# Attention and gated FFN on one core: the output tile moves into u's buffer, seven tiles for transposed scores, fetches asked for earlier, some squares on VectorE

## The chip, the cores and the metric

The kernel runs on one core of a Trainium2 chip. The metric is the device time of one execution in microseconds; smaller is better. The profile is of one execution, and its times are counted from the first instruction.

## The reference, cut to what matters

```python
# u, v: (4, 3136, 256)   z: (4, 3136, 64)   all float32
scores = (1 / S) * z @ z^T                  # per batch, S = 3136; symmetric
attn   = maximum(scores, 0) ** 2
x      = u * (attn @ v)                     # the input of the FFN
h      = maximum(x @ w_in, 0)               # 256 -> 1024
c      = conv over the sequence, 3 taps, per channel of h
out    = (h * sigmoid(c)) @ w_out           # 1024 -> 256
```

## The kernel before, in words

**Blocks and slots.** A batch of 3136 rows is cut into six query blocks of 512 (QB = 6, q = 0 to 5) and a rest of 64 rows. A block has 25 slots (NJ), one for each strip of 128 key rows. Four batches make 24 blocks and 600 slots; slot k lies in block k // 25. A slot makes a 128 x 512 tile of scores, squares its positive part, splits it into a rounded high part `ah` and a rest `al`, and TensorE multiplies both with v (`attend`, L431; six matmuls of 512 columns). The FFN of the block before runs in between (`ffn_*`, matmuls at L585 to L588 and L658 to L660).

**Three kinds of slot.** In a plain slot TensorE computes the scores (`scores`, L316 and L317, into the PSUM tile `s`), ScalarE takes the positive part into `t` (L391), VectorE multiplies the two (L402). A transposed slot uses that scores are symmetric: an earlier block has computed that tile, GpSimd has parted its words (`part`, L346), SP has written them to DRAM (`spill`, L359), and a transposing DMA brings them back into a tile `tp` (`fetch`, L367). There ScalarE squares `tp` twice: into the PSUM tile `s` (L388) and, rounded, into `ah` (L407); VectorE takes the difference (`al`, L155). The third kind are the four strips on a block's diagonal, at positions 1, 8, 15 and 22 of the block (2, 8, 15, 22 in the last block of a batch). The first of them is computed whole; the other three, called side pieces here, compute only the part right of the diagonal (384, 256 and 128 columns, L385) and get the part left of it by a transposing DMA from the DRAM tile `dd` of the same block (`fetch_side`, L375). The share of transposed slots grows with q: 16 of 25 in block 4 and 20 of 25 in block 5 of a batch.

**The order of the work** is written out by hand. In iteration k of the main loop the program issues, engine by engine and in this order: `split_hi` and `split_lo` of slot k+2, `relu` (with the squares above) of slot k+3, whatever the event table `ev` holds for k, `fetch` of slot k+LD, `fetch_side` of slot k+LE, `part` of slot k+2, `spill` of slot k+1, `attend` of slot k and `scores` of slot k+4. Each engine runs its own instructions in this order. All DMAs but two at the very end are issued by SP, one behind the other: one that must wait for a tile holds up all behind it.

**Rings of tiles.** The `tp` tiles form a ring of LB buffers, given out in the order of the program to `fetch` and `fetch_side` alike; a request gets the tile that was given out LB requests earlier and waits until that slot's last reader is done, which as a rule is `split_hi` of that slot, issued in iteration slot - 2. The PSUM tiles `s` are two: `scores` of slot k+4 must wait until `split_lo` (`al`, L155) has read the one given out two requests before. Of `ah` and `al` there are four each.

**u and the output.** `load_u` (L292) brings 512 KB of u for a block into the single tile `ut`; after the block's last slot `gate_x` multiplies the attention result into it (L553, L549) and `split_x` splits it for the FFN (`xh`, `xl`, L155 and L158). When the block's FFN is through, `evac` copies the output from PSUM into the single tile `ob` (ScalarE, L158), and `store` writes it out (L692). In the last blocks `tail` lists the work instead and orders it by its own costs; the rest of 64 rows of all batches (`r`) ends there with an `ob` of its own.

Of the kernel before, what the change touches and what calls it, by code (L numbers as in the profile page):

```python
# [8 lines left out]
F32 = mybir.dt.float32  # L9
# [5 lines left out]
AF = mybir.ActivationFunctionType  # L15
ALU = mybir.AluOpType
# [10 lines left out]


LA, LT, LS = 4, 3, 2
LD, LE, LP, LX, LB = 8, 5, 2, 1, 5  # L30
DG = [1, 8, 15, 22]


# [7 lines left out]
FS = [2, 5, 8, 11, 15, 18, 21, 24]  # L41
RELU, TAP, ST1, ST2, SIG, GATE, GHI, OUT0, OUT1 = 1, 2, 2, 3, 4, 4, 5, 10, 11
EVAC = 12
XS = 1

C_GATE, C_ST1, C_ST2, C_G, C_SIG, C_HI = 0, 2, 2, 2, 1, 3
# [22 lines left out]
def kernel(  # L69
# [10 lines left out]
    nc = tc.nc  # L80
# [4 lines left out]
    P = 128  # L85
    NB = 512
    QB = S // NB
# [3 lines left out]
    NJ = (S + P - 1) // P  # L91
    HALF = S - (NJ - 1) * P
    RW = B * (RQ + 3)
    NBLK = B * QB
    NS = NBLK * NJ
    DC = D // P
    FC = DFF // P
    SC1 = 2.0**-12
# [5 lines left out]
    wk = ctx.enter_context(tc.tile_pool(name="wk", bufs=1))  # L104
# [26 lines left out]
    def at_slot(k):  # L131
        blk, i = divmod(k, NJ)
        return blk, *ent[blk // QB][blk % QB][i]

    def side(k):
        blk, j, tr = at_slot(k)
        x = j - blk % QB * CB
        return x if blk and not tr and 0 <= x < CB else None
# [18 lines left out]
    def copy(eng, out, a):  # L157
        (eng.copy if eng is nc.scalar else eng.tensor_copy)(out, a)  # L158
# [128 lines left out]
    ut = {}  # L287
# [10 lines left out]
    sc, ah, al, pav = {}, {}, {}, {}  # L298

    def held(k):  # L300
        blk, j, _ = at_slot(k)
        return blk % QB == RB and j == NJ - 1
# [17 lines left out]
    rl, pl, dq, dd, tp = {}, {}, {}, {}, {}  # L320
# [57 lines left out]
    def relu(k):  # L378
        x = side(k)
        if at_slot(k)[2] or x or held(k):  # L380
            if held(k):
                tp[k] = rr.pop("s")
            if x:
                rl[k] = tp[k]
                nc.scalar.activation(tp[k][:, x * P :], sc[k][:, x * P : NB], AF.Relu, scale=SC1)  # L385
            else:
                sc[k] = ps.tile([P, 512], F32, tag="s", name="s", bufs=2)
            nc.scalar.activation(sc[k][:, :NB], tp[k], AF.Square, scale=SC1**-0.5)  # L388
            return
        rl[k] = wk.tile([P, NB], F32, tag="t", name="t", bufs=3)  # L390
        nc.scalar.activation(rl[k], sc[k][:, :NB], AF.Relu, scale=SC1)  # L391
        if act_squares(k):
            nc.scalar.activation(sc[k][:, :NB], rl[k], AF.Square, scale=SC1**-0.5)


    def act_squares(k):
        return SQ0 <= k < SQ1 and k % 2 == 1
# [174 lines left out]
    ph, hb, cc, gg, po = {}, {}, {}, {}, {}  # L572
# [4 lines left out]
    def width(blk):  # L577
        return RW - 2 if blk == "r" else NB
# [85 lines left out]
    ob = {}  # L664
# [7 lines left out]
    def evac(blk, dcs=range(DC), engs=(nc.scalar, nc.scalar)):  # L672
        e = width(blk)
        if blk not in ob:
            if blk == "r":
                ob[blk] = wk.tile([P, DC, RW], F32, tag="ut", name="ob", bufs=1)
            else:
                ob[blk] = wk.tile([P, DC, NB], F32, tag="ob", name="ob", bufs=1)
        for dc in dcs:
            copy(engs[dc], ob[blk][:, dc, :e], po[blk][dc][:, :e])  # L680

# [19 lines left out]
    PRE, MID, VEC, POST, PE0, PE1 = range(6)  # L701

    def at(slot, cls, fn, *args):
        ev[slot][cls].append((fn, args))
# [3 lines left out]
    for q in zs[2:]:  # L708
        s = min(C0.index(j) for j in range(q * CB, min(q * CB + CB, NJ))) - LA - 3
# [10 lines left out]
    for b in range(1, B):  # L720
        k0 = (b * QB - 1) * NJ
        for q in range(QB + 1):
            s = k0 - (QB - 2 - q) * NJ + (12 if q % 2 == 0 else 4)
            if q == QB - 2:
                s = k0 + 6
            elif q == QB - 1:
                s = k0 + NJ + 6
            elif q == QB:
                s = k0 + 9
            if b == 1 and q < 2:  # L730
                s = (Q0 - QB) * NJ + NJ + k0 + 4 + 8 * q
# [3 lines left out]
        for j in range(0, NJ, 2):  # L735
            s = k0 + max(last[j] + 2, last.get(j + 1, 0) + 2, V0 + V1 * j // NJ)
            if j == NJ - 1:
                s = k0 + V0 - 2
# [5 lines left out]
    n = len(RN) - 1  # L744
    for b in range(B):
# [9 lines left out]
        for i in range(n + 1):  # L755
            s = k5 + (R_J + 2 * i if i < n else R_D + 1) + 1
# [16 lines left out]
    for i, (_, what, f) in enumerate(sorted(need)):  # L773
        s = WS[i]
# [3 lines left out]
    for n in range(4):  # L778
        at(W_C + n, POST, prep_w, n, "conv", 0)
    for blk in range(NBLK):  # L780
        at(blk * NJ + 6, POST, load_u, blk)

    def before_end(slot, *args):
        if slot < NS:
            at(slot, *args)

    for blk in range(NBLK - 1):
        k0 = (blk + 1) * NJ
        at(k0, C_GATE, gate_x, blk, G)
        at(k0 + XS, C_XS, split_x, blk, (V, G))  # L790
        for f in range(FC):
            s = k0 + FS[f]
            if s == NS - 1:
                break
            at(s, POST, ffn_halo, blk, f)
            at(s, PE1, ffn_in, blk, f)
            at(s + RELU, C_RELU, ffn_relu, blk, f)
            at(s + RELU, C_RELU, ffn_keep, blk, f)
            at(s + TAP, C_TAP, ffn_tap, blk, f)
            at(s + ST1, C_ST1, ffn_conv, blk, f, 1)  # L800
            at(s + ST2, C_ST2, ffn_conv, blk, f, 2)
            before_end(s + SIG, C_SIG, ffn_sig, blk, f)
            before_end(s + GATE, C_G, ffn_gate, blk, f, G)
            before_end(s + GHI, C_HI, ffn_hi, blk, f, A)
            before_end(s + GHI, PE1, ffn_lo, blk, f, G)
            before_end(s + OUT0, PE0, ffn_out, blk, f, 0)
            before_end(s + OUT1, PE0, ffn_out, blk, f, 1)
        if blk < NBLK - 2:
            at(s + EVAC, C_EV, evac, blk)
            at(s + EVAC + 1, POST, store, blk)  # L810
    at(NS - 2, POST, rem_x)

    def tail():
# [43 lines left out]
        def end(w, d, engs, ds):  # L857
            n = width(w)
            out = []
            for dc in range(DC):  # L860
                c = op(engs[dc], 90 + n, d[dc::2], evac, w, [dc], [E[e] for e in engs])
                out.append(c)
                if ds:
                    op(ds[dc], 60, [c], store_half, w, dc, nc.sync if ds[dc] == "S" else nc.scalar)
            if not ds:
                op("S", 60, out, store, w)
            return out
# [44 lines left out]
    with tc.manual_schedule():  # L912
# [12 lines left out]
        for k in range(-LA, NS):  # L925
# [3 lines left out]
            if early and 0 <= k + LT:  # L929
                relu(k + LT)  # L930
                square(k + LT)
# [4 lines left out]
            if not early and k + LT < NS:  # L936
                relu(k + LT)
                square(k + LT)
# [67 lines left out]
```

## Time and profile before

| | |
|---|---|
| time, median of 3 runs | 1557.33 us (1556.37 to 1557.98) |
| time of the profiled execution | 1555.86 us |
| its span, first to last instruction | 1554.1 us |
| TensorE busy | 1531.0 us (99% of the span), 6796 matmuls |
| ScalarE busy | 1243.2 us (80%) |
| VectorE busy | 1055.6 us (68%) |
| GpSimd busy | 802.6 us (52%) |
| granted TensorE clock | 1.00 |

A line of the groups of instructions gives source line, engine, operation, tile written <- tiles read, shape, count, then the busy time in us and the mean of one in ns, and last the idle time of the engine just before them with what ended it. A matmul's own duration (some 390 ns for 512 columns) overlaps with the next, so the idle time of TensorE is the figure to read there. In a timeline the bracket at the end of a line is the idle time just before that instruction and what ended it.

### The profile page before, as it was taken

Reading aid. Unit: us, or ns where it says so; the run is one execution under the profiler, and the core shown is the slowest. Engines: PE = TensorE matmul, PEld = TensorE weight load, DVE = VectorE, ACT = ScalarE, POOL = GpSimd, SP = SyncE. Lnnn points to the kernel's source line nnn. Section 1 sums busy time; section 2 is a strip of 40 time slices with the busy share of each in tenths; the row PEclk is TensorE's granted clock in tenths of the full one; section 3 lists DMA queues with packets and bytes.
Section 4 is the critical chain, followed back from the end, with each engine's and each line's share of the span. In section 5 each row is a group of like instructions: output and inputs, shape, how many; then the busy total and the mean of one; then the engine's idle time right before and its main releaser. Section 6 shows DMA issues by size and latency. Waiting matters only on the chain.

```text
span 1554.1 us, 22492 instructions
## 1 busy us (share of the span) xinstructions
PE 1531.0 (99%) x6796; PEld 1259.6 (81%) x6796; DVE 1055.6 (68%) x1632; ACT 1243.2 (80%) x2365; POOL 802.6 (52%) x1121
## 2 busy tenths in 40 slices
PE   8999999999999999999999999999999999999998
PEld 6778888787888888887788888888788888888887
DVE  8997766556677766655767766665577776665557
ACT  8888788788777877878878777787787777878877
POOL 7765544346655543444765544444486553443333
PEclk9999999999999999999999999999999999999999
DMA  6543566675444556658344465574843445567431
GB/s 207 151 138 98 126 156 143 125 160 126 149 126 124 146 117 137 157 106 180 122 138 128 119 147 129 124 165 102 173 139 115 142 110 130 133 118 163 112 71 35
DMA packets 424650, 205.22 MB, mean 132 GB/s; under 512 B 317136, under 2 KB 404176, under 8 KB 424528
## 3 DMA queue, kind: packets, MB, share of 16 engines
q1 hardware_dynamic: 423856, 203.39, 53.3%
q8 instruction: 53, 0.87, 0.2%
q14 instruction: 69, 0.57, 0.1%
q10 hardware_dynamic: 672, 0.40, 0.1%
HBM read 36.59 MB, written 86.90 MB: 79 GB/s over the span
## 4 chain that ended last, share of the span: by engine, by line
PE 87%; ACT 6%; DMA 2%; POOL 2%; issue 1%; DVE 1%; SPq 0%; ACTq 0%; DVEq 0%; POOLq 0%
PE av L431 45%; PE ph L585 5%; PE ph L588 5%; PE ph L586 5%; PE o L660 5%; PE o L658 5%; PE o L659 5%; PE s L316 5%; PE s L317 4%; DMA tp<-dd 2%; PE av L498 2%; ACT s L388 1%; ACT ah L407 1%; ACT ph L622 1%; ACT hb L612 1%
## 5 line engine op out<-in xcount | busy, mean ns | idle before, releaser
L431 PE MATMUL av<-ah,vv 128*128 128x512 f32 x2400 | 736.7, 390 | 1.2 <-ACT ah L407 1.0
L155 DVE TENSOR_TENSOR al<-s,ah 128x512 fp32r<-128x512 f32 x576 | 397.0, 689 | 293.9 <-ACT ah L407 259.5
L431 PEld LDWEIGHTS av<-ah,vv 128*128 128x128 f32 x2400 | 449.7, 188 | 95.9 <-ACT re L509 1.7
L431 PE MATMUL av<-al,vv 128*128 128x512 f32 x1152 | 448.9, 390 | 0.5 <-DVE al L155 0.5
L155 POOL TENSOR_TENSOR gl<-hb,gh 128x512 fp32r<-128x512 f32 x192 | 248.2, 1293 | 166.0 <-ACT gh L158 165.8
L402 DVE TENSOR_TENSOR s<-s,t 128x512 f32<-128x512 f32 x295 | 205.5, 697 | 157.7 <-ACT t L391 156.7
L627 DVE SCALAR_TENSOR_TENSOR ph<-hb,cw,ph 128x512 f32<-128x512 f32 x384 | 286.6, 746 | 5.5 <-ACT ph L622 5.2
L346 POOL COPY pl<-t 128x1024 uint16<-128x1024 uint16 (+1 forms) x275 | 280.4, 1021 | 2.2 <-POOL hb L604 1.6
L431 PEld LDWEIGHTS av<-al,vv 128*128 128x128 f32 x1152 | 216.3, 188 | 47.2 <-DVE al L155 2.0
L391 ACT ACTIVATE t<-s 128x512 f32<-128x512 f32 x295 | 176.7, 599 | 93.6 <-PE s L317 84.6
L409 ACT CAST ah<-s 128x512 fp32r<-128x512 f32 x295 | 173.7, 589 | 72.9 <-DVE s L402 72.7
L388 ACT ACTIVATE s<-tp 128x512 f32<-128x512 f32 x301 | 179.3, 596 | 31.1 <-DMA tp<-dd 29.2
L617 POOL COPY halo<-hb 128x2 f32<-128x2 f32 x160 | 30.2, 189 | 318.9 <-ACT hb L612 318.9
L407 ACT ACTIVATE ah<-tp 128x512 fp32r<-128x512 f32 x301 | 188.7, 627 | 0.1
L316 PE MATMUL s<-zq,zh 128*128 128x512 f32 (+2 forms) x364 | 137.0, 376 | 16.1 <-DVE al L155 10.7
L585 PE MATMUL ph<-xh,wih 128*128 128x512 f32 x384 | 151.3, 394 | 0.6 <-DVE hb L641 0.6
L586 PE MATMUL ph<-xh,wil 128*128 128x512 f32 x384 | 150.0, 391 | 0.0
L658 PE MATMUL o<-gh,wol 128*128 128x512 f32 x384 | 149.5, 389 | 0.0
L659 PE MATMUL o<-gh,woh 128*128 128x512 f32 x384 | 149.5, 389 | 0.0
L660 PE MATMUL o<-gl,woh 128*128 128x512 f32 x384 | 149.4, 389 | 0.0
L634 ACT ACTIVATE ph<-ph 128x512 f32<-128x512 f32 (+1 forms) x200 | 115.4, 577 | 26.4 <-DVE ph L627 22.2
L641 DVE TENSOR_TENSOR hb<-ph,hb 128x512 f32<-128x512 f32 x192 | 131.8, 686 | 7.0 <-ACT ph L634 1.2
(117 smaller groups left out, 1871.5 us busy)
## 6 DMA issues: line engine op xcount, KB each, us to landing
dq<-pl SPq DMA_DIRECT2D x232, 256.0 KB, 2.8
vst<-in_v_dram SPq DMA_DIRECT2D x48, 256.0 KB, 3.3
ut<-in_u_dram SPq DMA_DIRECT2D x24, 512.0 KB, 4.2
out_dram<-ob SPq DMA_DIRECT2D x19, 512.0 KB, 3.3
st<-in_z_dram SPq DMA_DIRECT2D x24, 256.0 KB, 3.0
dd<-pl SPq DMA_DIRECT2D x23, 192.0 KB, 2.4
tp<-dq SPq DMA_TRANSPOSE x232, 3.7
dq<-pl SPq DMA_DIRECT2D x24, 128.0 KB, 2.4
```

The source lines that it names most:

```text
L155: eng.tensor_tensor(out=out, in0=a, in1=b.bitcast(F32), op=ALU.subtract)
L316: nc.tensor.matmul(s[:, c:], lhsT=zh[:, w], rhs=r, start=True, stop=False)
L346: nc.gpsimd.tensor_copy(pl[k], src.bitcast(U16).rearrange("p (n h) -> p h n", h=2))
L402: nc.vector.tensor_tensor(out=s, in0=s, in1=rl[k], op=ALU.mult)
L407: nc.scalar.activation(ah[k], tp.pop(k), AF.Square, scale=SC1**-0.5)
L431: nc.tensor.matmul(o, lhsT=w[:, j, d], rhs=r, start=first and i == 0, stop=last and i == len(ops) - 1)
L585: nc.tensor.matmul(o, lhsT=wih[:, dc, w], rhs=xh[blk][:, dc], start=(dc == 0), stop=False)
L586: nc.tensor.matmul(o, lhsT=wil[:, dc, w], rhs=xh[blk][:, dc], start=False, stop=False)
L627: nc.vector.scalar_tensor_tensor(out=c, in0=hb[blk, f][:, k : e + k], scalar=cw[:, f, k : k + 1], in1=c, op0=ALU.mult, op1=ALU.add,)
L658: nc.tensor.matmul(o, lhsT=wol[:, f, d], rhs=h, start=(f == 0), stop=False)
L659: nc.tensor.matmul(o, lhsT=woh[:, f, d], rhs=h, start=False, stop=False)
L660: nc.tensor.matmul(o, lhsT=woh[:, f, d], rhs=l, start=False, stop=(f == FC - 1))
```

## The change

The 4 KB per partition of `ob` are given up: `ob` becomes a tile of the ring `ut` (one buffer), and the two KB tiles of `tp` become seven instead of five. For that, `load_u` moves from slot 6 of its block to slot 18, and `store` from one slot behind `evac` to two. The output of the rest rows, which had used the ring `ut`, takes a tile of the ring `hb`. `fetch` is asked for ten slots ahead instead of eight, `fetch_side` six instead of five. In blocks 4 and 5 of each batch, for odd slots, VectorE computes the square of `tp` in place of ScalarE: `scalar_tensor_tensor` with both inputs `tp`; these are 80 instructions in all. TensorE and GpSimd keep their instructions in the same order.

```diff
-LD, LE, LP, LX, LB = 8, 5, 2, 1, 5
+LD, LE, LP, LX, LB = 10, 6, 2, 1, 7
 ...
+UL = 18
+DS = 4
 ...
-            nc.scalar.activation(sc[k][:, :NB], tp[k], AF.Square, scale=SC1**-0.5)
+            if by_vector(k):
+                nc.vector.scalar_tensor_tensor(
+                    out=sc[k][:, :NB], in0=tp[k], scalar=SC1**-1, in1=tp[k], op0=ALU.mult, op1=ALU.mult
+                )
+            else:
+                nc.scalar.activation(sc[k][:, :NB], tp[k], AF.Square, scale=SC1**-0.5)
 ...
+    def by_vector(k):
+        return k // NJ % QB >= DS and k % 2 == 1
 ...
             if blk == "r":
-                ob[blk] = wk.tile([P, DC, RW], F32, tag="ut", name="ob", bufs=1)
+                t = wk.tile([P, NB + 32], F32, tag="hb", name="or", bufs=3)
+                ob[blk] = t[:, : DC * RW].rearrange("p (a n) -> p a n", a=DC)
             else:
-                ob[blk] = wk.tile([P, DC, NB], F32, tag="ob", name="ob", bufs=1)
+                ob[blk] = wk.tile([P, DC, NB], F32, tag="ut", name="ob", bufs=1)
 ...
-        at(blk * NJ + 6, POST, load_u, blk)
+        at(blk * NJ + UL, POST, load_u, blk)
 ...
-            at(s + EVAC + 1, POST, store, blk)
+            at(s + EVAC + 2, POST, store, blk)
```

The first place is SP's queue in block 5 of the first batch, around the DMA of its second side piece, slot 140 (`tp<-dd` with 512 columns; the digits behind `dq` only tell DRAM tiles apart). Before:

```order
L359 DMA dd<-pl 256x1x256
L208 DMA vst<-in_v_dram 128x2x256
L521 DMA_TRANSPOSE rt<-do 128x4x256
L367 DMA_TRANSPOSE tp<-dq_386 128x1x1024 x2
L208 DMA vst<-in_v_dram 128x2x256
L367 DMA_TRANSPOSE tp<-dq_386 128x1x1024
L375 DMA_TRANSPOSE tp<-dd 128x1x512
L367 DMA_TRANSPOSE tp<-dq_386 128x1x1024
L692 DMA out_dram<-ob 128x2x512
```

And with the change:

```order
L361 DMA dd<-pl 256x1x256
L210 DMA vst<-in_v_dram 128x2x256
L531 DMA_TRANSPOSE rt<-do 128x4x256
L369 DMA_TRANSPOSE tp<-dq_384 128x1x1024 x2
L377 DMA_TRANSPOSE tp<-dd 128x1x512
L210 DMA vst<-in_v_dram 128x2x256
L369 DMA_TRANSPOSE tp<-dq_384 128x1x1024 x2
L210 DMA vst<-in_v_dram 128x2x256
L703 DMA out_dram<-ob 128x2x512
```

The side piece's DMA stands ahead of one more load of v and one more fetch, and the store of the output stands further behind it. The fetches ahead of it belong to slots two later than before.

The second place is VectorE at the start of that block 5. Before:

```order
L155 TENSOR_TENSOR al<-s,ah 128x512
L627 SCALAR_TENSOR_TENSOR ph<-hb,cw,ph 128x512
L155 TENSOR_TENSOR xl<-ut,xh 128x512
L155 TENSOR_TENSOR al<-s,ah 128x512
L627 SCALAR_TENSOR_TENSOR ph<-hb,cw,ph 128x512
L155 TENSOR_TENSOR al<-s,ah 128x512
L641 TENSOR_TENSOR hb<-ph,hb 128x512
```

And with the change:

```order
L157 TENSOR_TENSOR al<-s,ah 128x512
L391 SCALAR_TENSOR_TENSOR s<-tp 128x512
L637 SCALAR_TENSOR_TENSOR ph<-hb,cw,ph 128x512
L157 TENSOR_TENSOR xl<-ut,xh 128x512
L157 TENSOR_TENSOR al<-s,ah 128x512
L637 SCALAR_TENSOR_TENSOR ph<-hb,cw,ph 128x512
L157 TENSOR_TENSOR al<-s,ah 128x512
L391 SCALAR_TENSOR_TENSOR s<-tp 128x512
L651 TENSOR_TENSOR hb<-ph,hb 128x512
```

In every second slot the square `s<-tp` stands right behind a slot's `al` and ahead of the FFN's steps; ScalarE's queue loses the same squares (L388) at the same places.

## Rows read from the trace of the kernel before

**Rows 1.** The page, part 1: busy us (share of the span) and instructions.
```profile
PE 1531.0 (99%) x6796; PEld 1259.6 (81%) x6796; DVE 1055.6 (68%) x1632; ACT 1243.2 (80%) x2365; POOL 802.6 (52%) x1121
```
**Rows 2.** Waits of PE, whole span: us in total, times, longest us.
```profile
PE s L316 <- DVE al L155: 10.7, 9, 1.8
PE av L431 <- ACT ah L407: 1.0, 1, 1.0
```
**Rows 3.** The same view, stretch 65 to 130 us alone.
```profile
PE s L316 <- DVE al L155: 1.1, 2, 0.7
```
**Rows 4.** Timeline of PE, end of the first three batches: start, us, instruction, idle before.
```profile
354.99 0.33 PE L316 MATMUL s<-zq,zh 128*128 128x128 f32 x1 [1.52 <-DVE al L155]
364.06 0.50 PE L316 MATMUL s<-zq,zh 128*128 128x512 f32 x1 [1.76 <-DVE al L155]
...
735.38 0.33 PE L316 MATMUL s<-zq,zh 128*128 128x128 f32 x1 [1.70 <-DVE al L155]
743.77 0.50 PE L316 MATMUL s<-zq,zh 128*128 128x512 f32 x1 [1.07 <-DVE al L155]
...
1116.57 0.33 PE L316 MATMUL s<-zq,zh 128*128 128x128 f32 x1 [1.73 <-DVE al L155]
1124.60 0.50 PE L316 MATMUL s<-zq,zh 128*128 128x512 f32 x1 [0.72 <-DVE al L155]
```
**Rows 5.** Timeline of ACT in the same three places.
```profile
342.35 0.60 ACT L388 ACTIVATE s<-tp 128x512 f32<-128x512 f32 x1 [3.77 <-DMA tp<-dd]
358.95 0.60 ACT L388 ACTIVATE s<-tp 128x512 f32<-128x512 f32 x1 [2.55 <-DMA tp<-dd]
...
722.73 0.60 ACT L388 ACTIVATE s<-tp 128x512 f32<-128x512 f32 x1 [4.05 <-DMA tp<-dd]
738.66 0.60 ACT L388 ACTIVATE s<-tp 128x512 f32<-128x512 f32 x1 [1.87 <-DMA tp<-dd]
...
1103.90 0.60 ACT L388 ACTIVATE s<-tp 128x512 f32<-128x512 f32 x1 [5.55 <-DMA tp<-dd]
1119.49 0.60 ACT L388 ACTIVATE s<-tp 128x512 f32<-128x512 f32 x1 [1.51 <-DMA tp<-dd]
```
**Rows 6.** The page, part 5: groups of instructions.
```profile
L388 ACT ACTIVATE s<-tp 128x512 f32<-128x512 f32 x301 | 179.3, 596 | 31.1 <-DMA tp<-dd 29.2
L627 DVE SCALAR_TENSOR_TENSOR ph<-hb,cw,ph 128x512 f32<-128x512 f32 x384 | 286.6, 746 | 5.5 <-ACT ph L622 5.2
```
**Rows 7.** Timeline of SP, block 5 of the first batch.
```profile
338.60 1.20 SPq L375 DMA_TRANSPOSE tp<-dd  x1
```
**Rows 8.** DMA issues: count, KB each where known, median us to landing.
```profile
out_dram<-ob SPq DMA_DIRECT2D x19, 512.0 KB, 3.3
...
tp<-dd SPq DMA_TRANSPOSE x69, 3.0
```
**Rows 9.** Stretches: us, then busy us (x) of PE, PEld, DVE, ACT, POOL; clock, DMA share, GB/s.
```profile
312.00:375.00 63.00, 59.72 (x263) 48.56 (x262) 36.39 (x56) 52.20 (x101) 29.28 (x44) 1.00 0.65 142
```
**Rows 10.** Instructions on tile ut: duration ns min/median/max, first and last start.
```profile
L155 DVE TENSOR_TENSOR xl<-ut,xh x25: 676/691/694, 61.1 to 1509.9; 128x512 fp32r<-128x512 f32 x25
...
L549 POOL TENSOR_TENSOR ut<-x,ut x23: 1289/1296/1306, 57.7 to 1445.9; 128x512 f32<-128x512 f32 x23
L155 POOL TENSOR_TENSOR xl<-ut,xh x23: 1302/1467/1877, 61.1 to 1457.1; 128x512 fp32r<-128x512 f32 x23
...
DMA to landing us min/median/max: 3.7/4.2/6.1
```
**Rows 11.** Line 531, all of it: duration ns min/median/max.
```profile
L531 DVE SCALAR_TENSOR_TENSOR xr<-rt,ur x4: 343/348/363, 347.3 to 1486.6; 128x128 f32<-128x128 f32 x4
```
**Rows 12.** Timeline, block 4 of the second batch: PE at slot 265, VectorE before it.
```profile
654.18 0.28 PE L316 MATMUL s<-zq,zh 128*128 128x256 f32 x1
```
**Rows 13.** Timeline of DVE, the same place.
```profile
652.97 0.69 DVE L155 TENSOR_TENSOR al<-s,ah 128x512 fp32r<-128x512 f32 x1
...
655.00 0.69 DVE L155 TENSOR_TENSOR al<-s,ah 128x512 fp32r<-128x512 f32 x1 [0.68 <-ACT ah L407]
```

## The prediction
> **What bounds the kernel now.** I read the page first, then TensorE's waits, then the timelines of the places where it waits. TensorE is busy for 1531.0 of 1554.1 us [rows 1], and the change leaves its instructions as they are, so the only time to be had is TensorE's idle time. Most of what is recorded as a wait behind the program's start has one name: `scores` (L316) waits for `al` (L155), nine times, 10.7 us, and once `attend` waits for `ah`, 1.0 us [rows 2]. Two of the nine, 1.1 us, lie in the stretch from 65 to 130 us where the weights are prepared [rows 3]; the change hardly touches that. That leaves 10.7 - 1.1 + 1.0 = 10.6 us. Six of these waits come in pairs at the ends of the first three batches: 1.52 and 1.76, 1.70 and 1.07, 1.73 and 0.72 us, together 8.50 [rows 4].
>
> VectorE is late with `al` there because ScalarE was late with `ah`, and ScalarE was late because it stood still for a side piece: each pair on TensorE has a pair on ScalarE ahead of it, in which L388 waits for `tp<-dd` [rows 5]. The first of a pair is slot 15 of block 5 (3.77, 4.05, 5.55 us), the second slot 22 (2.55, 1.87, 1.51). The second ones fit to the hundredth: 2.55 - 1.76 = 0.79, 1.87 - 1.07 = 0.80, 1.51 - 0.72 = 0.79. So the engines are 0.8 us ahead there, and what a side piece is later than that TensorE loses. For the first ones it is 2.25 and 2.35; in the third batch, with the `ah` wait of 1.0 us counted in, about 2.8. All waits of L388 for side pieces make 29.2 us in the span [rows 6]; the 9.9 us not shown lie where TensorE was far enough behind, but for one in block 4 of the first batch that makes the seventh `al` wait, 9.6 - 8.50 = 1.1 us.
>
> **Why the side pieces are late.** One slot takes (743.77 - 364.06) / 150 = 2.53 us (those two are the scores of slots 150 and 300) [rows 4]. Take slot 140, the first pair's piece. SP asks for it in iteration 135. Five requests back in the ring is slot 138, and that tile comes free with `split_hi` in iteration 136; the piece is wanted by `relu` in iteration 137. So one slot, 2.53 us, is left for a DMA that ScalarE sees 342.35 - 338.60 = 3.75 us after its issue [rows 5, 7], and whose median landing is 3.0 us [rows 8]. Counting all 69 side pieces in this way, with SP's order, 12 have one slot and 57 have two; slot 22 of block 5 has two and is still late when SP lags.
>
> **The change, part by part.** *Ring of seven, fetches 10 and 6 ahead.* Slot 140 is asked for in iteration 134, gets the tile of slot 133 (free since iteration 131), and stands in SP's queue behind the fetch of slot 144, which needs the tile of slot 137, free in iteration 135. So it starts two slots ahead of its use instead of one. The same count for all 69 gives one slot more for 65 and two more for 4 (slot 22 of each block 4, where the seventh wait comes from). A slot is 2.53 us, so the first waits become 3.77 - 2.53 = 1.24, 1.52 and 3.02 us, the second ones 0.02, 0 and 0. Against the margins 2.25, 2.35 and 2.8 only the third batch could still lose, 0.2 us; against 0.8 none. Earlier fetches of `dq` tiles only lengthen a lead that shows no wait.
>
> *Squares on VectorE.* 80 x 0.596 = 47.7 us leave ScalarE [rows 6], about 10 squares or 6 us in each of eight blocks, three of them between slots 15 and 22, so the margin of the first waits grows by up to 1.8 us. VectorE's price shows nowhere in the trace: no such instruction has both inputs 512 columns wide in SBUF. From below it is the 0.69 us of `xl<-ut,xh`, two SBUF inputs of that size in a plain `tensor_tensor` [rows 10]; from above 4 x 0.348 = 1.39 us, since the one form that does match (L531) takes 348 ns for 128 columns [rows 11] and that includes a fixed part. I take 0.75, the same operation on 512 columns with PSUM operands [rows 6]. 80 x 0.75 = 60 us, 7.5 in a block in which VectorE is busy for 36.39 of 63 us [rows 9]; it lies beside TensorE's work and I cost it at nothing. If that cover were gone, the tightest place says what it costs: `al` ends at 652.97 + 0.69 = 653.66 and the scores that need it start at 654.18, 0.52 us later [rows 12, 13].
>
> *Output in u's ring, load_u at slot 18, store one later.* The new order is `gate_x` and `split_x` of one block (slots 0 and 1 of the next), `evac` at slot 11, `store` at 13, `load_u` at 18, use at 25. `evac` has ten slots of room. `load_u` waits for a store that lands in 3.3 us [rows 8] and was issued 5 slots, 12.7 us, before; its own landing takes 6.1 us at most [rows 10] of the 7 slots, 17.7 us, to its use. Nothing. The store one slot later keeps SP from standing at an `evac` that has not run yet; a small gain, already contained in the leads. In the tail, the last outputs wait for tiles that were free long before; nothing. Taking 512 KB out of the first 20 us may gain or lose some tenths; I put it at zero with 0.5 us on each side.
>
> **The sum.** 10.6 us of waits, less 0.2 that may stay in the third batch and 0.4 for new small waits, is 10.0 us. The profiled execution took 1555.86 us, so 1545.9 us; the median of the runs shown is 1.47 us above that execution, so I predict **1547.3 us**. About 0.2%, 3.1 us, is what a measurement of this kernel can tell from no change.
>
> **The rivals.** *Half of it stays.* The count above follows the tiles; SP must also keep up. Its transposing DMAs take 1.2 us of issue each [rows 7], and a fetch that stands ahead of a side piece now needs its own tile first. If the pieces gain half a slot only, the waits fall by 1.27 us: 2.50, 2.78 and 4.28 against margins of 2.25 to 2.8 plus what ScalarE is spared. Then the second waits, 1.28, 0.60 and 0.24, lose 0.5 once, and the first at most 0.25, 0.43 and 1.5. With some new waits of the squares this is 3 to 5 us left, 1550 to 1552 us. Chance 0.13.
>
> *ScalarE itself is short.* If it is not the DMA but ScalarE's load, 52.20 of 63 us in block 5 [rows 9], that makes TensorE wait, the pieces come earlier and the waits only change their name; with 6 us less to do it would still keep perhaps 2 us. 1555.5 us, within 0.2%. Against it stands the fit to 0.01 us with the DMA waits. That VectorE's added squares give back what the pieces gain comes out at the same time. Chance 0.08.
>
> *The squares collide with GpSimd: slower.* In the trace GpSimd's `xl<-ut,xh`, which runs beside VectorE's instruction on the same tiles, takes 1302 to 1877 ns, its `ut<-x,ut`, of the same kind and size, 1289 to 1306 [rows 10]; so an instruction with two SBUF inputs on VectorE can cost GpSimd up to 0.58 us. In the other direction, a square that starts behind a GpSimd instruction could stand for up to 1.3 us. The mechanism: square and wait, 0.75 + 1.3, push the next `al` back by 2.05 us; of that 0.52 us of margin and some 0.68 us in which VectorE waits for `ah` anyway [rows 12, 13] take up 1.2, and TensorE loses 0.85 at a slot that computes scores. From a delay of 1.2 us on it decides. At two such slots in each of 8 blocks that is 13.6 us, and 1547.3 + 13.6 = 1560.9 us. The Trainium skill ("SBUF — State Buffer", section "Who interferes with whom") states the rule: a VectorE instruction with two SBUF inputs contends with a GpSimd instruction that reads SBUF, and whichever comes second is blocked until the first is done. By that rule, the trace agrees for GpSimd as the second; no row here shows VectorE blocked for that long. Against it: GpSimd is busy for 29.28 of 63 us [rows 9], so most squares meet nothing or the end of something, and VectorE idles for over 26 us of those 63. Chance 0.04.
>
> **How the numbers follow.** The forecast has 0.75; the three rivals 0.13, 0.08 and 0.04. Around the forecast lie the half microsecond of the start on each side, the 0.6 taken off the waits, and 1 us by which the runs shown differ: 1544.5 to 1549.5 (below, if the 0.6 and the waits of the weight stage go too). To hold 8 in 10 the range takes in the half case: 1544.5 to 1553.0. Faster by over 0.2% is below 1554.2: the forecast and the half case, less a little, 0.86. Within 0.2%: 0.10. Slower: 0.04.
>
> **What would show it.** Right: `scores` waiting for `al` falls from 10.7 us to below 2, with nothing but the two waits in the weight stage and some tenths left; ScalarE's waits for `tp<-dd` fall from 29.2 us to below 8 (a part may turn up as waits of VectorE, which now squares slot 22's piece); a new group of 80 squares `s<-tp` on VectorE of 0.69 to 0.80 us; ScalarE's busy time is 48 us lower. Wrong: squares of over 1 us, or idle time ahead of them that ends with GpSimd; TensorE waiting for `al` at new places in blocks 4 and 5; `gate_x` waiting for the DMA of u; or the pairs of waits at the ends of the batches still there.

## The result and the profile after

The changed kernel takes 1541.16 us (median of 4 runs, 1540.89 to 1541.77) against 1556.85 us before: a ratio of 0.990, 95% interval 0.9883 to 0.9917, 15.7 us faster. The forecast was 1547.3 us with a range of 1544.5 to 1553.0: the direction was right, the gain 10.0 us instead of 15.7, and the time lies 3.3 us below the range. The profiled executions, 1555.86 and 1540.89 us, differ by 15.0 us, and that is the difference that can be taken apart.

TensorE's waits of the changed kernel, in the view of [rows 2] (us in total, times, longest):

```profile
PE s L318 <- DVE zq L157: 5.2, 1, 5.2
PE s L318 <- DVE al L157: 1.2, 2, 0.7
PE ph L595 <- DVE hb L651: 0.9, 1, 0.9
PE av L441 <- DVE al L157: 0.5, 1, 0.5
PE av L441 <- ACT x L558: 0.5, 1, 0.5
PE s L318 <- DVE wr L277: 0.2, 1, 0.2
```

Of the nine waits for `al` two are left, 1.2 us; they are the two of the weight stage [rows 3]. The first line is the start of the program. Neither ScalarE nor VectorE has a wait for `tp<-dd` left, where ScalarE had 29.2 us [rows 6]; ScalarE's squares, and the new ones of VectorE, as groups of instructions:

```profile
L395 ACT ACTIVATE s<-tp 128x512 f32<-128x512 f32 x221 | 132.2, 598 | 1.8
```

```profile
L391 DVE SCALAR_TENSOR_TENSOR s<-tp 128x512 f32<-128x512 f32 x80 | 65.6, 820 | 6.9 <-ACT tp L387 6.6
```

The first is the line of [rows 6] with 80 instructions and 47.1 us fewer, and no DMA ends its idle time any more. ScalarE's busy time as a whole fell by 38.8 us only, where 48 was foreseen, since the drawn bars of neighbours overlap. The second group took 820 ns on average, where 750 was assumed. The same six matmuls as in [rows 4], in the timeline of the changed kernel:

```profile
351.00 0.22 PE L318 MATMUL s<-zq,zh 128*128 128x128 f32 x1
358.04 0.39 PE L318 MATMUL s<-zq,zh 128*128 128x512 f32 x1
...
727.10 0.22 PE L318 MATMUL s<-zq,zh 128*128 128x128 f32 x1
734.13 0.39 PE L318 MATMUL s<-zq,zh 128*128 128x512 f32 x1
...
1103.15 0.22 PE L318 MATMUL s<-zq,zh 128*128 128x128 f32 x1
1110.19 0.39 PE L318 MATMUL s<-zq,zh 128*128 128x512 f32 x1
```

None has idle time in brackets. The distances to [rows 4] are 3.99, 6.02, 8.28, 9.64, 13.42 and 14.41 us: the gain comes mostly in steps at the ends of the batches, where the waits were. The stretch with the same 263 matmuls as in [rows 9], block 5 of the first batch, which now takes 3.8 us less:

```profile
309.69:368.85 59.16, 59.16 (x263) 48.73 (x262) 44.04 (x67) 47.03 (x90) 32.05 (x44) 1.00 0.64 142
```

TensorE is busy for all of it. VectorE went from 36.39 to 44.04 us, ScalarE from 52.20 to 47.03, and GpSimd from 29.28 to 32.05, though GpSimd has the same 44 instructions.

### The profile page after: what moved, and what is told of

Same layout as the page of the kernel before. It is cut to its first block, busy times and chain, and to the rows that moved or that the text cites. A ratio compares the mean times of both kernels' runs of the same rounds, so it can differ in the third digit from the quotient of the medians.

```text
span 1539.1 us, 22577 instructions
## 1 busy us (share of the span) xinstructions
PE 1526.2 (99%) x6796; PEld 1260.3 (82%) x6796; DVE 1110.6 (72%) x1712; ACT 1204.4 (78%) x2285; POOL 822.5 (53%) x1121
## 4 chain that ended last, share of the span: by engine, by line
PE 95%; DVE 2%; ACT 1%; issue 1%; DMA 0%; POOL 0%; DVEq 0%; ACTq 0%; POOLq 0%
PE av L441 50%; PE ph L595 6%; PE o L670 6%; PE o L668 6%; PE o L669 6%; PE ph L596 6%; PE ph L598 6%; PE s L318 5%; PE s L319 5%; PE av L508 1%; DVE s L412 0%; DVE al L157 0%; DVE ph L637 0%; ACT t L398 0%; DMA st<-in_z_dram 0%
## 5 line engine op out<-in xcount | busy, mean ns | idle before, releaser
L157 POOL TENSOR_TENSOR gl<-hb,gh 128x512 fp32r<-128x512 f32 x192 | 252.0, 1313 | 157.5 <-ACT gh L160 157.1
L622 ACT ACTIVATE hb<-ph 128x512 f32<-128x512 f32 x192 | 114.7, 597 | 40.3 <-PE ph L598 39.0
```

Of the source, the lines that this page charges most:

```text
L157: eng.tensor_tensor(out=out, in0=a, in1=b.bitcast(F32), op=ALU.subtract)
```

## The experiments

Theory A says that the gain comes from side pieces that are ready earlier; B, that it comes from ScalarE's squares; C, from the moved u, output and store; D, from fetches ten ahead. Each kernel was timed in three rounds beside the kernel before.

**Without the squares on VectorE.** `DS = 4` becomes `DS = 6`.

> The changed kernel with all squares of transposed tiles back on ScalarE. Theory A (the gain comes from the side pieces, which start one slot earlier): within 2 us of the changed kernel, 1541 to 1543 us, and ScalarE's waits for tp<-dd stay below 8 us. Theory B (ScalarE's load made TensorE wait, and the squares on VectorE are the gain): the pairs of waits at the ends of the first three batches come back, 1551 to 1556 us. Theory C (the freed order: output in u's ring, u loaded later, store later): 1541 us, as A.

1541.78 us (1541.08 to 1542.02), ratio 0.9905 [0.989, 0.992], and no wait for `tp<-dd`. B falls as the main cause: the squares are worth 0.6 us here by the medians, and the runs of the two kernels overlap.

**Side pieces five ahead.** `LE` from 6 back to 5.

> The changed kernel with the side pieces asked for five slots ahead as before; ring of seven, fetches ten ahead, squares on VectorE as changed. By the count of tiles 8 pieces have one slot again and 61 have two. Theory A: ScalarE or VectorE waits for tp<-dd again at slot 15 of block 5 (2 to 4 us each), and part of the gain goes: 1545 to 1553 us. Theory B: 1541 us. Theory C: 1541 us.

1541.18 us (1540.79 to 1542.96). A's number was wrong. The waits at slot 15 are back, but shorter than before, and TensorE feels little of them. ScalarE's waits in this run:

```profile
ACT s L395 <- DMA tp<-dd: 8.1, 4, 2.3
```

Four waits of some 2 us, all at slot 15 of block 5; at slot 22 none. In the ring of seven that piece takes the tile of slot 143, not 144, so the ring alone gives it a slot more. The count was right for slot 15 and had missed that for slot 22. TensorE in the first and the third batch, where ScalarE's waits are 2.08 and 2.32 us:

```profile
351.91 0.33 PE L318 MATMUL s<-zq,zh 128*128 128x128 f32 x1 [0.26 <-DVE al L157]
1104.96 0.33 PE L318 MATMUL s<-zq,zh 128*128 128x128 f32 x1 [0.52 <-DVE al L157]
```

Ahead of these two late `al` VectorE ran a square of 0.95 and 0.96 us, so the squares may have a part in them; how large a part was not tried.

**The old ring.** `LD, LE, LB` back to 8, 5, 5.

> The changed kernel with LD, LE and LB as before (8, 5, 5): what is left of the change are the squares on VectorE and the moves of u, output and store. Theory A: the waits for tp<-dd are back and most of the gain is gone, 1549 to 1556 us, better than before only by what ScalarE is spared. Theory B: 1541 us. Theory C: 1541 us.

1556.47 us (1553.07 to 1559.44, ten runs), ratio 0.9999 [0.9986, 1.0012]: nothing of the gain is left, though squares and moves are in, and A's range ends 0.5 us lower. Squares and moves together give nothing with the old ring; that could still be two effects of opposite sign, which the next two runs separate.

**The squares alone.**

```diff
-            nc.scalar.activation(sc[k][:, :NB], tp[k], AF.Square, scale=SC1**-0.5)
+            if k // NJ % QB >= 4 and k % 2 == 1:
+                nc.vector.scalar_tensor_tensor(
+                    out=sc[k][:, :NB], in0=tp[k], scalar=SC1**-1, in1=tp[k], op0=ALU.mult, op1=ALU.mult
+                )
+            else:
+                nc.scalar.activation(sc[k][:, :NB], tp[k], AF.Square, scale=SC1**-0.5)
```

> The kernel before with the 80 squares on VectorE and nothing else. Theory A: as the run with the old ring, 1549 to 1556 us. Theory B: 1541 us. Theory C: no gain, 1556 us; the distance to the run with the old ring is what the moves are worth.

1552.82 us (1550.6 to 1553.89), 0.9972 [0.9962, 0.9983]: 3.9 us of gain, while ScalarE and VectorE still wait for `tp<-dd`. So the squares make up for late pieces in part. That this is better than the run before, which has the moves as well, suggests that the moves cost some 3.7 us with the old ring.

**The moves alone.** The changed kernel with 8, 5, 5 and `DS = 6`.

> The changed kernel with the old ring and leads (8, 5, 5) and the squares back on ScalarE: only u's and the output's tile, u's load at slot 18 and the store one slot later are left. Theory A, as it stands after the first runs (the moves put u's load beside the side pieces and cost some 3 us as long as those have no room; ring and leads give the room): 1557 to 1561 us. Theory C (the moves are a gain of their own): 1541 to 1550 us.

1561.03 us (1560.19 to 1564.5), 1.003 [1.0018, 1.0041]: slower by 4.0 us. C is not only without gain, its sign is the other one.

**Fetches eight ahead.** `LD` from 10 back to 8.

> The changed kernel with fetches of transposed tiles eight slots ahead as before, ring of seven, side pieces six ahead: every side piece has at least four slots between its tile and its use. Theory A: 1540 to 1542 us, no wait for tp<-dd at all. A rival, D (it is the fetches ten ahead, tp<-dq, that gain): 1550 to 1556 us.

1540.55 us (1540.22 to 1541.03), one wait for `tp<-dd` of 0.3 us. D falls: the fetches ten ahead gain nothing.

**The kernel before with side pieces six ahead.** One number: `LE` from 5 to 6.

> The kernel before with one number changed: side pieces asked for six slots ahead instead of five; ring of five, fetches eight ahead. By the count of tiles slots 8 and 15 of block 5 get two slots instead of one, slot 22 of block 4 three, slot 22 of block 5 stays at two. Theory A (each piece late for itself): the first wait of each pair goes, the second stays, 1548 to 1551 us. Theory A2 (the second wait of a pair is the echo of the first, since SP and the ring stand still with ScalarE): both go, 1541 to 1546 us. Theory D: no gain, 1556 us.

1542.65 us (1542.2 to 1543.09), 0.9909 [0.9892, 0.9925]. One number in the old kernel gives 14.4 of the 15.7 us. The time lies in A2's range, not in A's. Its timeline of ScalarE at the places of [rows 5]:

```profile
338.34 0.60 ACT L388 ACTIVATE s<-tp 128x512 f32<-128x512 f32 x1 [1.25 <-DMA tp<-dd]
353.85 0.60 ACT L388 ACTIVATE s<-tp 128x512 f32<-128x512 f32 x1 [1.32 <-DMA tp<-dd]
...
715.59 0.60 ACT L388 ACTIVATE s<-tp 128x512 f32<-128x512 f32 x1 [2.03 <-DMA tp<-dd]
730.27 0.60 ACT L388 ACTIVATE s<-tp 128x512 f32<-128x512 f32 x1 [0.62 <-DMA tp<-dd]
...
1091.77 0.60 ACT L388 ACTIVATE s<-tp 128x512 f32<-128x512 f32 x1 [1.81 <-DMA tp<-dd]
1106.22 0.60 ACT L388 ACTIVATE s<-tp 128x512 f32<-128x512 f32 x1 [0.40 <-DMA tp<-dd]
```

At slot 15 the prediction had 1.24, 1.52 and 3.02 us for one slot more; measured are 1.25, 2.03 and 1.81. TensorE's waits for `al` are the two of the weight stage, 1.2 us. The 1.32 us at slot 22 cost TensorE nothing that the profile records, so the margin of 0.8 us is no constant; that it holds only behind a longer wait at slot 15, which has used up the lead, fits the rows but was not tried. The count of tiles gave slot 22 no slot more, and its wait fell all the same: asked for one iteration earlier, its DMA goes out ahead of the two stores `zq<-zh` and `zq<-zl` (at 349.88, they at 351.21 and 351.81), which before went ahead of it (353.73 and 354.31, it at 355.01).

**One side piece of each batch earlier.** The kernel before, with slot 15 of block 5 alone asked for six ahead.

```diff
-            if 0 <= k + LE < NS:
-                fetch_side(k + LE)
+            for d in (LE + 1, LE):
+                if 0 <= k + d < NS and (late_one(k + d) == (d > LE)):
+                    fetch_side(k + d)
...
+    def late_one(k):
+        return k // NJ % QB == RB and k % NJ == 15
```

> The kernel before, in which only the side piece at slot 15 of block 5 of each batch is asked for one slot earlier; four DMAs move in the whole program. Theory A: three waits of TensorE go (1.52, 1.70, and 1.01 + 1.73 us with what they cost beyond), 1549 to 1551 us. Theory A2: the second waits go as well, 1545 to 1547 us. Theory D: no gain, 1556 us.

1548.11 us (1546.66 to 1548.44), 0.9942 [0.9927, 0.9957], between the two expectations and nearer to A's. The first and the second wait of the first batch, on ScalarE:

```profile
340.82 0.60 ACT L391 ACTIVATE s<-tp 128x512 f32<-128x512 f32 x1 [2.07 <-DMA tp<-dd]
357.95 0.60 ACT L391 ACTIVATE s<-tp 128x512 f32<-128x512 f32 x1 [3.08 <-DMA tp<-dd]
```

and TensorE there:

```profile
363.05 0.50 PE L316 MATMUL s<-zq,zh 128*128 128x512 f32 x1 [2.24 <-DVE al L155]
```

TensorE's first wait, 1.52 us [rows 4], is gone, its second is 2.24 us instead of 1.76. The piece at slot 22 is late for itself, not as an echo: A2 falls, although its number was right for the run before. A's number there had missed that `LE` moves the second piece too.

**Ring of seven without squares.** The changed kernel with `LE = 5` and `DS = 6`.

> The changed kernel with side pieces five ahead as before and all squares on ScalarE: ring of seven and fetches ten ahead remain, and the moves. By the count, slot 22 of blocks 4 and 5 has three slots, slot 15 of block 5 one, as before. Theory A (a piece costs TensorE what it is later than a margin of 2.25 to 2.8 us at slot 15, 0.8 us at slot 22): waits of some 2 us at slot 15 lie inside the margin, 1541 to 1544 us. If the squares on VectorE are what gives the margin: the stalls at slot 22 come back, 1546 to 1551 us.

1542.31 us (1541.45 to 1542.79). The waits at slot 15 are there, 6.1 us in four times, 2.2 at the longest, and TensorE's wait view shows none for them. So 2.2 us is about the margin without the help of the squares, as [rows 4, 5] had given 2.25; behind the longest, TensorE's next matmul began 0.33 us after the one before instead of the usual 0.23.

**u's load late, and the store late, each alone in the kernel before.** `load_u` at slot 18 instead of 6; `EVAC + 1` to `EVAC + 2`.

> The kernel before with u's load at slot 18 instead of 6 and nothing else. If this is the move that costs (512 KB and one issue right ahead of the side piece at slot 22): 1559 to 1562 us. If not: 1556 to 1557.5 us.

> The kernel before with the store one slot later and nothing else. If this is the move that costs (SP then stands at the store when the fetches behind it are already due): 1559 to 1562 us. If SP standing at the store made side pieces late, as the prediction had it: a gain, 1553 to 1556 us. If it does nothing: 1556 to 1557.5 us.

u late: 1555.01 us (1553.7 to 1557.33), 0.9985 [0.9976, 0.9995], if anything 2.1 us of gain. Store late: 1563.48 us (1562.02 to 1565.97), 1.0041 [1.0025, 1.0057], 6.4 us slower and 1.5 us above the expected range. SP's queue in the run with the late store, first batch:

```profile
347.77 0.47 SPq L692 DMA_DIRECT2D out_dram<-ob  x1
...
357.52 1.25 SPq L375 DMA_TRANSPOSE tp<-dd  x1
```

and in the kernel before, the same two DMAs:

```profile
341.19 0.57 SPq L692 DMA_DIRECT2D out_dram<-ob  x1
...
355.01 1.26 SPq L375 DMA_TRANSPOSE tp<-dd  x1
```

In the kernel before the store goes out at 341.19, while SP stands for a free tile anyway. One slot later in the program it stands behind that tile's fetch: it goes out 6.6 us later, among fetches that are already due, and the side piece of slot 22 behind them starts 2.5 us later. ScalarE and TensorE then:

```profile
360.74 0.60 ACT L388 ACTIVATE s<-tp 128x512 f32<-128x512 f32 x1 [3.74 <-DMA tp<-dd]
```

```profile
365.84 0.80 PE L316 MATMUL s<-zq,zh 128*128 128x512 f32 x1 [3.32 <-DVE al L155]
366.43 0.63 PE L317 MATMUL s<-zq,zl 128*128 128x512 f32 x1
366.86 0.63 PE L585 MATMUL ph<-xh,wih 128*128 128x512 f32 x1
```

against waits of 2.55 and 1.76 us before [rows 4, 5]. Not all of the 6.4 us is waiting: these matmuls begin 0.43 us apart, where 0.23 is usual, and the stretch that they lie in shows why (columns as in [rows 9], the granted clock third from the end):

```profile
365.41:368.82 3.41, 2.98 (x7) 2.43 (x8) 2.72 (x5) 1.87 (x4) 1.83 (x3) 0.50 0.00 0
```

TensorE had waited 1.71 us, worked for 7.3 us and waited another 3.32 us; towards the end of that last wait its granted clock fell from 1.00 to 0.50, the lower of its two levels (1.2 GHz), and it rose again after 3.41 us of which it worked for most. A second such stretch (1123.17 to 1126.58) begins behind a wait of 1.72 us. By the spacing of the matmuls one stretch costs up to 1.6 us (an estimate), less where a later wait shrinks for it.

**Side pieces six ahead and the squares, in the kernel before.** Two parts of the change; ring, fetches and moves are the old ones.

> The kernel before with side pieces six ahead and the 80 squares on VectorE: two parts of the change without ring, fetches and moves. Theory A: the run with six alone (1542.65 us) less what the squares are worth once nothing waits for side pieces, 0.6 us by the difference of the changed kernel to the run without them: 1541 to 1542.5 us. If ring or fetches hold a gain of their own: above 1542.5 us.

1540.92 us (1540.73 to 1541.58), 0.9896 [0.9878, 0.9914]: as fast as the whole change, and 1.7 us faster than six ahead alone, where 0.6 was expected for the squares. Ring, fetches and moves together add nothing to these two. This run, the one with fetches eight ahead (1540.55) and the changed kernel (1541.16) differ by no more than their runs do; none beats the others.

## Why the prediction was right, and where it failed

**Right: the place and the mechanism.** TensorE waited for `al`, that for ScalarE, and that for `tp<-dd`; a slot more of lead for the side pieces takes these waits away. The run with one number changed shows it alone. How much earlier the pieces come was not right: the waits of 1.24, 1.52 and 3.02 us that ScalarE was to keep at slot 15 are 0 in the changed kernel, and 1.25, 2.03 and 1.81 in the run with one number changed, so the agreement of the first is luck. The DMA of slot 140 shows it:

```profile
332.89 1.14 SPq L377 DMA_TRANSPOSE tp<-dd  x1
```

Before, it went out at 338.60 [rows 7], and followed matmul by matmul TensorE's work there is 2.31 us ahead now; so it goes out 3.4 us earlier in the work, not 2.53. The margin at slot 15 was about right: waits of up to 2.07 us cost nothing in the kernel before with one piece earlier; with the squares in, 2.08 us cost a recorded 0.26.

**Wrong: "The sum. 10.6 us of waits, less 0.2 that may stay in the third batch and 0.4 for new small waits, is 10.0 us."** A recorded wait was taken for the time that it costs. Between the scores of slots 147 and 150 the kernels move apart by 6.02 - 3.99 = 2.03 us for 1.76 us of recorded wait; in the second batch by 9.64 - 8.28 = 1.36 for 1.07, in the third by 14.41 - 13.42 = 0.99 for 0.72. Each of these waits costs 0.27 to 0.29 us more than its bracket. The timeline of TensorE before shows why; first four matmuls in steady work:

```profile
602.88 0.39 PE L431 MATMUL av<-ah,vv 128*128 128x512 f32 x1
603.10 0.39 PE L431 MATMUL av<-al,vv 128*128 128x512 f32 x1
603.33 0.39 PE L316 MATMUL s<-zq,zh 128*128 128x512 f32 x1
603.56 0.39 PE L317 MATMUL s<-zq,zl 128*128 128x512 f32 x1
```

and the one behind the wait at 364.06 [rows 4]:

```profile
364.39 0.40 PE L317 MATMUL s<-zq,zl 128*128 128x512 f32 x1
```

In steady work a matmul begins 0.23 us after the one before, but is drawn for 0.39. The bracket counts from the end of the drawn bar, so 0.16 us of every wait lie under it; and the first matmul behind a wait keeps the next one off for 0.33 us instead of 0.23, another 0.10. Both kernels run the same 6796 matmuls in the same order, so the distance between them can be followed across each of the eight waits: together they cost 13.1 us where the brackets say 10.6. This is 2.5 us of the miss, and part of why TensorE's busy time fell by 1531.0 - 1526.2 = 4.8 us although it does the same work.

**The rest of the 15.0 us.** Of the 0.6 us held back for new waits, 0.3 came, where `ph` waits for `hb` near the end of the program. Some 0.5 us are the squares, priced at "nothing": followed matmul by matmul, the executions with squares on VectorE gain 0.14 to 0.18 us at one place in each of the last three batches that those without do not. 0.4 us lie in the first 11 us of the program, where no edit changes the work and the executions profiled here differ by up to 1.0 us. Another 0.4 us each lie at the rest rows' 25 matmuls in the first and the last batch, below what the wait view lists. The first of them is also gone with the one number changed, and still there with one piece earlier, which fits the late piece of block 4; what makes the second was not tried. About 0.5 us of the 15.0 is not placed.

**Also mis-sized: "the median of the runs shown is 1.47 us above that execution".** After the change it is 0.3 us above, and 1.2 us of the miss are this. The runs of before spread over 4.3 us (1554.7 to 1559.0 in 17 runs), those of the old ring over 6.4; the changed kernel's over 0.9, and those of the other kernels without waits of TensorE at the ends of the batches over 0.8 to 1.4. The spread went with the waits. One way from the one to the other is the clock seen in the run with the late store. The profiled executions with u late and with the moves alone have such stretches too, two and one; all five begin towards the end of a wait of 1.7 to 3.5 us or within 1.4 us behind it, though other waits as long (2.24 us with one piece earlier) have none behind them. The profiled executions of before and after have none before their last matmuls. Of the 39 executions of the kernel before that were timed beside the experiments, 22 list a mean granted clock of 0.998 or less, of the changed kernel's four none. For the old ring the executions at 0.999 and above took 1553.1 to 1555.4 us, the others 1556.0 to 1559.4. For the kernel before the two groups overlap, so the clock is not shown to be all of its spread.

**"Nothing" for the moves** holds only under the new lead. That the late store "keeps SP from standing" had the wrong sign: alone it costs 6.4 us. The moves, meant to make room for the ring, need the new lead; the lead does not need the ring.

**The rivals.** Half of it stays: no, all went. ScalarE itself is short: the squares alone gain 3.9 us, so its load counts while pieces are late, but 0.6 us in the changed kernel, where they are not. The collision with GpSimd came and, in the changed kernel, made no wait of TensorE. A timeline of the changed kernel, GpSimd and VectorE:

```profile
333.70 1.30 POOL L157 TENSOR_TENSOR gl<-hb,gh 128x512 fp32r<-128x512 f32 x1
334.10 1.46 DVE L391 SCALAR_TENSOR_TENSOR s<-tp 128x512 f32<-128x512 f32 x1
334.93 0.67 POOL L614 COPY hb<-halo 128x2 f32<-128x2 f32 x1
```

GpSimd's subtraction ends at 335.00, and the square, which began behind it, at 335.56: it stood for some 0.7 us. The copy of two columns that GpSimd starts next, 188 ns in the median, stands for the end of the square. All squares of over 703 ns begin while a GpSimd instruction runs; the 28 that begin beside none take 681 to 703. The rule of the Trainium skill ("SBUF — State Buffer", section "Who interferes with whom") thus holds in both directions here. Over the 80 squares it is small:

```profile
L391 DVE SCALAR_TENSOR_TENSOR s<-tp x80: 681/754/1461, 245.4 to 1485.0; 128x512 f32<-128x512 f32 x80
```

The least is the lower bound of 0.69 us. That the median is the 0.75 us that was taken is luck, since it is a free square of 0.69 plus some waiting. The worst takes twice that, and ten take over 1 us, which the prediction had named as a sign of being wrong; VectorE still idles for 15 of 59 us in block 5, and no wait of TensorE followed in this kernel.

## What to carry to other kernels

Count, for each prefetch into a ring, the slots between the release of the tile it reuses (and of the tiles of requests ahead of it in its queue) and its first use, and hold that against the transfer's time: here requests with one slot of lead, and others behind them in the queue, made most of TensorE's avoidable waits, and one number moved them. Price a recorded TensorE wait at its bracket plus what lies under the last bar and behind the restart, here some 0.27 us. The store that went out where its queue stood anyway cost nothing to be seen here; one slot later in the program it cost 6.4 us.

## What was not expected

Three edits that look like parts of one plan have different signs alone (late store 6.4 us slower, squares 3.9 us faster, late u at most 2 us faster), and two of the parts, six ahead and the squares, already give the whole gain without the buffer that the rest was made for. And waits of some microseconds in a few places went together with the spread of the run times, 4.3 us with them and 0.9 without, and in some executions with stretches of half the clock behind them.
